# Splitting x's first block earlier, three values in an old constant tile, and weight decoding spread evenly after attention, in a fused attention and two-MLP kernel

## The chip, the cores and the metric

The kernel runs on one core of a Trainium2 chip. The metric is the device time of one execution in microseconds (us): the time before is the median of three runs, 884.39 us (883.90 to 886.73). About 0.3% is what a measurement of this kernel can tell from no change.

## The reference

Attention with a causal mask and a linear memory (4 batches, 8 heads, 576 tokens, 64 dimensions) makes a matrix x of 2304 tokens by 512. Two MLPs follow, everything in float32:

```python
x = attn_out.transpose(0, 2, 1, 3).reshape(B * S, H * D)   # 2304 x 512
h = x @ w_in                                               # 512 -> 2048
g = s * np.maximum(h, 0) ** 2 + b
y = g @ w_out                                              # 2048 -> 512
h = y @ w2_in                                              # 512 -> 1024
solu = h * softmax(h)
ln = (solu - mean) / sqrt(var + 1e-6) * g_ln
out = ln @ w2_out                                          # 1024 -> 512
```

## The kernel before, in words

**Products in three matmuls.** A float32 operand is split into a high part (fp32r, the faster matmul type) and a low rest. Each product is then three matmuls: high by high, low by high, high by low. In `hidden` (lines 420 to 438) the weights stand still in the array and x's parts `xh` and `xl` are streamed past them. In `ystep` (lines 602 to 610) weights stand still and `gh`, `gl` are streamed. In the second MLP it is `yh`/`yl` and `zh`/`zl` that stand still, and weights that are streamed (lines 665 to 667 and 728 to 730).

**Weights are decoded on the fly.** There are 48 weight tiles, numbered in the order of the list `order` (lines 114 to 118): w0 to w9 are the input and output weights of feature blocks f = 0 to 4, w10 to w31 are those of f = 5 to 15 in pairs (input of f, output of f), w32 to w39 belong to the second MLP's input, w40 to w47 to its output. `decode(n)` (lines 141 to 168) loads a tile, rebuilds its value in several integer steps (ACT line 152, DVE lines 153, 154, 156, 158, POOL line 159) and splits it (ACT line 163, DVE line 164). That is two ACT instructions, five on DVE, one on POOL and one load in SP's queue. `decode_to(n)` decodes up to tile n. Where the program calls it decides where in the order these instructions stand.

**Where tiles lie.** A pool is opened on the left side of the on-chip memory unless it says `side="right"`. Left, one behind the other: `const`, `wpA` (18 weight buffers), `dec`, the first part's pools, later `yT`, `yp` and the second MLP's pools. Right: attention's pools and, once attention is done, `wpB` (7 weight buffers), `xs2` (x, xh, xl of the second part) and `gs2` (r, gh, gl). `in_b` (line 135) says which weights go to `wpB`: w18 to w24 and w43 to w47. All others lie in `wpA`. In the built program every left tile behind `const` that a matmul reads begins at a multiple of 64 bytes, and every right one at 32 bytes past such a multiple.

**Stages.** Attention runs over 16 pairs of heads. Between its steps go pieces of the first part (`first_part`, f = 0 to 4 for each half batch of 288 tokens: five `h` tiles, then four `y` tiles, named h3_1_4 for batch 3, half 1, f = 4). What is left of it when attention ends, about 21 pieces, is emitted in the loop of lines 567 to 569, one decode behind each piece until tile 25. Then `second_part` runs f = 5 to 15 over five token blocks (four of 512 tokens, one of 256) in ten rounds: rounds 0 to 4 for f = 5 to 9, rounds 5 to 9 for f = 10 to 15. Each round loads its x (`load2`), splits it (`split_x`: four ACT and four DVE instructions), and alternates `hstep` and `ystep`. The decodes within rounds are spread by the lines 616 to 626. The second MLP ends the kernel.

**What sets the order.** The program is recorded in that order, and a scheduler (`schedule_with_timeline_sim=True`) then orders each engine's instructions by its own estimate of times. Each engine executes its list strictly in that order. `tc.issue_after(ins)` keeps an instruction from standing ahead of `ins` in that planning. Line 588 uses it: round 0's split may stand only behind the last ACT instruction of the first part (`lastact`, line 475). Line 630 allocates three tiles of one column for the first softmax of the second MLP in `const`.

Of the kernel before, what the change touches and what calls it, by code (L numbers as in the profile page):

```python
# [8 lines left out]
F32 = mybir.dt.float32  # L9
# [3 lines left out]
AF = mybir.ActivationFunctionType  # L13
# [4 lines left out]
P = 128  # L18
# [5 lines left out]
def attention_mlp_kernel(  # L24
# [9 lines left out]
    nc = tc.nc  # L34
# [65 lines left out]
    RA = 2 * FP1 + 8  # L100
    RB = 25 - RA
# [73 lines left out]
    def decode_to(n):  # L175
        while decoded[0] < min(n, NW):
            with tc.issue_after(mark[0]) if mark[0] else nullcontext():
                decode(decoded[0])
            decoded[0] += 1
# [235 lines left out]


    attended = [False]
    lastact = [None]

    def hidden(w, xh, xl, n, ps, r, gh, gl, square=False):  # L420

# [18 lines left out]
    def split_x(x, xh, xl):  # L440
        for c in range(NC):
            nc.scalar.activation(xh[:, c], x[:, c], AF.Copy)  # L442
            nc.vector.tensor_tensor(xl[:, c], x[:, c], xh[:, c].bitcast(F32), ALU.subtract)  # L443
# [3 lines left out]
    def first_part(b, pools):  # L447

        xs, gs, ys, _ = pools
        for sub in range(2):  # L450
            nm = f"{b}_{sub}"
            x = xbs[b][:, :, sub * N1:(sub + 1) * N1]
            xh = xs.tile([P, NC, N1], F32R, tag="xh", name=f"xh{nm}")
            xl = xs.tile([P, NC, N1], F32R, tag="xl", name=f"xl{nm}")
            split_x(x, xh, xl)
            gq = []
            for f in range(FP1):
                ps = pools[3][0].tile([P, 512], F32, tag="mh"[len(pools[3]) - 1], name=f"h{nm}_{f}")
                r = gs.tile([P, N1], F32, tag="r", name=f"r{nm}_{f}", bufs=2)
                g = gs.tile([P, 2, N1], F32R, tag="g", name=f"g{nm}_{f}")  # L460
                decode_to(f + 1)
                hidden(wtiles["in", f], xh, xl, N1, ps[:, 0:N1], r, g[:, 0], g[:, 1])
                gq.append(g)
                yield
            for c in range(NC):
                ps = pools[3][-1].tile([P, 512], F32, tag="m", name=f"y{nm}_{c}")
                o = ps[:, 0:N1]
                decode_to(2 * FP1)
                for f in range(FP1):
                    wc = [wtiles["out", f][:, t, c * P:(c + 1) * P] for t in range(2)]  # L470
                    nc.tensor.matmul(o, wc[0], gq[f][:, 0], start=(f == 0), stop=False)
                    nc.tensor.matmul(o, wc[1], gq[f][:, 0], start=False, stop=False)
                    nc.tensor.matmul(o, wc[0], gq[f][:, 1], start=False, stop=(f == FP1 - 1))
                y = ys.tile([P, N1], F32, tag="y", name=f"yo{nm}_{c}")
                lastact[0] = nc.scalar.activation(y, o, AF.Copy).ins
                t0 = b * S + sub * N1
                nc.sync.dma_start(yd[:, c, t0:t0 + N1], y)
                yield
# [19 lines left out]
    with ExitStack() as fctx:  # L498
        xp = fctx.enter_context(tc.tile_pool(name="xp", bufs=2))
        xs = fctx.enter_context(tc.tile_pool(name="xs", bufs=1))  # L500
        gs = fctx.enter_context(tc.tile_pool(name="gs", bufs=FP1 + 1))
        ys = fctx.enter_context(tc.tile_pool(name="ys", bufs=2))
        ps_m = fctx.enter_context(tc.tile_pool(name="ps_m", bufs=2, space=PSUM))
        fpools = [xs, gs, ys, [ps_m]]
        filler = []
        with ExitStack() as actx:
            at = Attention(actx, xp)
            NS = CF + 1
            G = NU * NS
            at.load(0, "kq")  # L510
            warm_up(16)
            load_gate()
            at.load(1, "kq")
            at.load(0, "q", "z", "v")
            at.phi(0)
            at.load(1, "q", "v")
            load_consts()
            LAG = 2
            FG = NPAIR * NS + LAG + 1
            debt = 0.0  # L520
            tiles_of = lambda i: (2 * i, 2 * i + 1) if i < CF else (2 * CF,)
            for g in range(G + LAG):
                u, i = divmod(g, NS)
                if g < G and i != 1:
                    at.scores(u, *((0, 1) if i == 0 else (i,)))
                if g < 4:
                    with tc.issue_after(at.last):
                        warm_up(6)
                if i == CF and u < NU:
                    at.load(u + 2, "kq")  # L530
                if i == 3 and u < NU:
                    at.load(u + 2, "q")
                    at.load(u + 1, "z")
                if i == 2 and 0 < u < NU:
                    at.phi(u)
                if i == 3 and u < NU:
                    at.gates(u)
                if i == CF and u < NU:
                    at.weigh(u)
                if 0 <= g - LAG:  # L540
                    lu, li = divmod(g - LAG, NS)
                    for t in tiles_of(li):
                        at.transposes(lu, t)
                    if li == CF - 1:
                        at.recip_t(lu)
                        at.phi_t(lu)
                    if li == CF:
                        at.values(lu)
                        at.load(lu + 2, "v")
                        if lu % NPAIR == NPAIR - 1:  # L550
                            filler.append(first_part(lu // NPAIR, fpools))
                decode_to(min(int(g / 3.4), RA))
                if filler and g >= FG:
                    debt += 0.93 * 6 * (FP1 + NC) / (G - FG)
                    while debt >= 1 and filler:
                        debt -= 1
                        if next(filler[0], 0) == 0:
                            filler.pop(0)
        wpools[1] = ctx.enter_context(tc.tile_pool(name="wpB", bufs=RB, side="right", reuse_waits="tile"))
        xs2 = pctx.enter_context(tc.tile_pool(name="xs2", bufs=1, side="right", reuse_waits="tile"))  # L560
        gs2 = pctx.enter_context(tc.tile_pool(name="gs2", bufs=2, side="right", reuse_waits="tile"))
        ps_y = pctx.enter_context(tc.tile_pool(name="ps_y", bufs=1, side="right", space=PSUM, reuse_waits="tile"))
        ps_h = pctx.enter_context(tc.tile_pool(name="ps_h", bufs=2, side="right", space=PSUM, reuse_waits="tile"))
        fpools[3] = [ps_h, ps_m]
        load2(0, False)
        attended[0] = True
        for it in filler:
            for _ in it:
                decode_to(min(decoded[0] + 1, RA + RB))

    def second_part():
        load2(0, True)
# [4 lines left out]
        for ri, (fs, bi) in enumerate(rounds):  # L577
# [7 lines left out]
            x = xq.pop(ri)  # L585
            xh = xs2.tile([P, NC, NB], F32R, tag="xh", name=f"xh2_{ri}")
            xl = xs2.tile([P, NC, NB], F32R, tag="xl", name=f"xl2_{ri}")
            with tc.issue_after(lastact[0]) if ri == 0 else nullcontext():
                split_x(x[:, :, 0:n], xh[:, :, 0:n], xl[:, :, 0:n])
            ys = [ps_y.tile([P, 512], F32, tag=f"y{c}", name=f"y2_{ri}_{c}") for c in range(NC)]  # L590
            gq = {}

# [19 lines left out]
            for i, f in enumerate(fs):  # L612
                hstep(f)
                if i >= 1:
                    ystep(fs[i - 1])
                step += 1
                if ri == 0:
                    decode_to(min(decoded[0] + 2, g2))
                elif ri < len(blocks):

                    decode_to(g2 + (late - g2) * step // steps)
                elif ri < last:

                    decode_to(late + (last2 - late) * step // steps)
                else:
                    decode_to(decoded[0] + 1)
                if ri == last and i == 2:

                    z = dec.tile([P, WN, 2], I32, tag="raw", name="z0").rearrange("p n t -> p (n t)").bitcast(F32)
                    first["z"] = weights_of(0, z, *(const.tile([P, 1], F32, name=f"t0_{k}") for k in range(3)))  # L630
            if ri == last:
                decode_to(NW)
                first[1] = products(1)
# [36 lines left out]
    def weights_of(t, z, mx, sm, mu):  # L670

        hh = products(t) if t not in first else first.pop(t)
        nc.vector.tensor_reduce(mx, hh, AX.X, ALU.max, negate=True)
        nc.scalar.activation(z, hh, AF.Exp, bias=mx, accum_out=sm)
        nc.vector.tensor_scalar(sm, sm, 1e-9, None, ALU.add)
        nc.vector.reciprocal(sm, sm)
        nc.vector.scalar_tensor_tensor(z, hh, sm, z, ALU.mult, ALU.mult, accum_out=mu)
        return z, mu
# [119 lines left out]
```

## Time and profile before

| | before |
|---|---|
| median of 3 runs | 884.39 us |
| the profiled execution | 885.48 us |
| its span, first to last instruction | 883.7 us |
| PE (matmul) busy | 850.8 us, 96% of the span |
| DVE busy | 539.9 us, 61% |
| ACT busy | 513.7 us, 58% |
| POOL busy | 182.8 us, 21% |
| mean granted TensorE clock | 0.997 |

The span is 1.8 us shorter than the execution's own time. "Busy" of PE is a modelled figure: matmuls overlap, and the last one's end is estimated. So the text counts from the start of one matmul to the start of the next. "Idle before" in a row names what released the engine.

### The profile page before, as it was taken

To read this page: it belongs to the slowest core of one execution; us is meant where nothing else is said; L and a number is where in the kernel's file an instruction comes from. 1 tells how busy PE (TensorE), PEld (TensorE's weight loads), DVE (VectorE), ACT (ScalarE), POOL (GpSimd) and SP (SyncE) were. 2 spreads that over 40 slices of the span, in tenths; PEclk is the share of its full clock that TensorE was granted. 3 is DMA by queue.
4 is the path that set the end of the run, shared out by engine and by line. 5 is a ranking of instruction groups with operands and counts; after the bars stand their busy time and mean duration, and the time that the engine had idled before them with its cause. 6 is when DMAs were issued, how large, how long until landed. Compare 5 with 4: busy or idle time off the path is not lost.

```text
span 883.7 us, 14245 instructions
## 1 busy us (share of the span) xinstructions
PE 850.8 (96%) x5344; PEld 699.0 (79%) x5344; DVE 539.9 (61%) x1236; ACT 513.7 (58%) x1094; POOL 182.8 (21%) x180
## 2 busy tenths in 40 slices
PE   7899889999999999899999999999999999999997
PEld 5677668888878878878888888888988888888885
DVE  3898986768778467922338864454775444454532
ACT  4776765666666665555558776556774333433332
POOL 4445351332333222200002311101120000000000
PEclk9999999999999999999999999999999999999999
DMA  7445242533343204472013422111200000000000
GB/s 228 133 148 184 79 155 59 155 97 119 115 149 118 69 1 156 147 263 95 3 45 114 144 100 96 48 48 55 89 24 1 25 25 23 13 24 24 25 25 36
DMA packets 41494, 76.44 MB, mean 86 GB/s; under 512 B 6352, under 2 KB 20176, under 8 KB 41424
## 3 DMA queue, kind: packets, MB, share of 16 engines
q1 hardware_dynamic: 41424, 75.52, 26.5%
q8 instruction: 42, 0.69, 0.3%
q14 instruction: 28, 0.23, 0.1%
HBM read 61.35 MB, written 14.16 MB: 85 GB/s over the span
## 4 chain that ended last, share of the span: by engine, by line
PE 78%; DVE 13%; ACT 3%; issue 2%; POOL 1%; DMA 1%; POOLq 0%; SPq 0%; ACTq 0%; DVEq 0%
PE h L424 7%; PE h L425 7%; PE h L426 7%; PE y L609 5%; PE y L608 5%; PE y L610 5%; PE h L665 4%; PE h L666 4%; PE h L667 4%; PE o L730 4%; PE o L729 4%; PE o L728 4%; PE pp L372 3%; PE s L315 3%; PE po L404 3%
## 5 line engine op out<-in xcount | busy, mean ns | idle before, releaser
L425 PE MATMUL h<-xl,w 128*128 128x512 f32 (+2 forms) x380 | 131.0, 345 | 2.1 <-DVE xl L443 2.1
L159 POOL TENSOR_TENSOR wa<-wa,raw 128x512 f32<-128x512 f32 x48 | 67.8, 1415 | 314.5 <-DVE raw L158 198.2
L424 PE MATMUL h<-xh,w 128*128 128x512 f32 (+2 forms) x380 | 130.0, 349 | 2.8 <-ACT xh L442 2.5
L426 PE MATMUL h<-xh,w 128*128 128x512 f32 (+2 forms) x380 | 129.2, 341 | 0.0
L427 ACT ACTIVATE r<-h 128x512 f32<-128x512 f32 (+2 forms) x95 | 45.6, 489 | 87.3 <-PE h L426 73.0
L298 ACT ACTIVATE pr<-pr,mx 128x128 f32<-128x128 f32 (+3 forms) x128 | 70.8, 555 | 37.5 <-DVE mx L331 37.5
L432 DVE TENSOR_TENSOR gl<-r,gh 128x512 fp32r<-128x512 f32 (+1 forms) x55 | 37.2, 685 | 88.1 <-ACT r L431 88.0
L424 PEld LDWEIGHTS h<-xh,w 128*128 128x128 f32 x380 | 70.9, 188 | 15.2 <-ACT xh L442 3.5
L425 PEld LDWEIGHTS h<-xl,w 128*128 128x128 f32 x380 | 71.5, 188 | 13.1 <-DVE xl L443 3.8
L608 PE MATMUL y<-gh,w 128*128 128x512 f32 (+1 forms) x220 | 80.8, 372 | 0.0
L609 PE MATMUL y<-gh,w 128*128 128x512 f32 (+1 forms) x220 | 80.8, 372 | 0.0
L426 PEld LDWEIGHTS h<-xh,w 128*128 128x128 f32 x380 | 71.5, 188 | 8.1 <-issue 0.4
L331 DVE CUSTOM_DVE_ANT_0 pr<-s,big 128x128 f32<-128x128 f32 (+3 forms) x128 | 56.2, 485 | 9.6 <-PE s L315 9.2
L375 ACT ACTIVATE pt<-pp 128x256 f32<-128x256 f32 (+2 forms) x96 | 47.2, 518 | 22.5 <-PE pp L372 22.0
L610 PE MATMUL y<-gl,w 128*128 128x512 f32 (+1 forms) x220 | 60.0, 372 | 0.0
L728 PE MATMUL o<-w,zh 128*128 128x512 f32 x144 | 56.8, 395 | 0.8 <-ACT zh L722 0.8
L730 PE MATMUL o<-w,zl 128*128 128x512 f32 x144 | 56.9, 395 | 0.6 <-DVE zl L723 0.6
L667 PE MATMUL h<-w,yl 128*128 128x512 f32 x144 | 56.6, 393 | 0.0
L729 PE MATMUL o<-w,zh 128*128 128x512 f32 x144 | 56.6, 393 | 0.0
L665 PE MATMUL h<-w,yh 128*128 128x512 f32 x144 | 56.6, 393 | 0.0
L666 PE MATMUL h<-w,yh 128*128 128x512 f32 x144 | 56.6, 393 | 0.0
L315 PEld LDWEIGHTS s<-kq 64*128 64x128 f32 x640 | 40.1, 187 | 19.3 <-issue 6.7
(142 smaller groups left out, 1959.1 us busy)
## 6 DMA issues: line engine op xcount, KB each, us to landing
raw<-in_moe_w_in_dram SPq DMA_DIRECT2D x24, 512.0 KB, 3.8
raw<-in_moe_w_out_dram SPq DMA_DIRECT2D x24, 512.0 KB, 3.5
kq<-in_kq_dram SPq DMA_DIRECT2D x16, 608.0 KB, 4.0
xr<-xd SPq DMA_DIRECT2D x8, 1024.0 KB, 5.9
q<-in_q_dram SPq DMA_DIRECT2D x16, 320.0 KB, 3.0
v<-in_v_dram SPq DMA_DIRECT2D x16, 320.0 KB, 3.1
xd<-xb SPq DMA_DIRECT2D x4, 1152.0 KB, 6.5
yd<-yo SPq DMA_DIRECT2D x32, 144.0 KB, 2.4
```

The lines of the kernel that those rows point to most:

```text
L424: nc.tensor.matmul(ps, wc[0], xh[:, c, 0:n], start=(c == 0), stop=False)
L425: nc.tensor.matmul(ps, wc[0], xl[:, c, 0:n], start=False, stop=False)
L426: nc.tensor.matmul(ps, wc[1], xh[:, c, 0:n], start=False, stop=(c == NC - 1))
L608: nc.tensor.matmul(o, wc[0], gh[:, 0:n], start=(f == fs[0]), stop=False)
L609: nc.tensor.matmul(o, wc[1], gh[:, 0:n], start=False, stop=False)
L610: nc.tensor.matmul(o, wc[0], gl[:, 0:n], start=False, stop=(f == fs[-1]))
L665: nc.tensor.matmul(o, yh[:, c], w[:, 0], start=(c == 0), stop=False)
L666: nc.tensor.matmul(o, yh[:, c], w[:, 1], start=False, stop=False)
L667: nc.tensor.matmul(o, yl[:, c], w[:, 0], start=False, stop=(c == NC - 1))
L728: nc.tensor.matmul(oo, zh, w[:, 0], start=(f == 0), stop=False)
L729: nc.tensor.matmul(oo, zh, w[:, 1], start=False, stop=False)
L730: nc.tensor.matmul(oo, zl, w[:, 0], start=False, stop=(f == NF2 - 1))
```

## The change

```diff
@@ -415,7 +415,6 @@
     attended = [False]
-    lastact = [None]
 
@@ -472,7 +471,7 @@ first_part
                 y = ys.tile([P, N1], F32, tag="y", name=f"yo{nm}_{c}")
-                lastact[0] = nc.scalar.activation(y, o, AF.Copy).ins
+                nc.scalar.activation(y, o, AF.Copy)
@@ -564,9 +563,11 @@
         attended[0] = True
+        turn = 0
         for it in filler:
             for _ in it:
-                decode_to(min(decoded[0] + 1, RA + RB))
+                turn += 1
+                decode_to(min(decoded[0] + (turn % 4 == 0), RA + RB))
@@ -585,8 +586,7 @@ second_part
-            with tc.issue_after(lastact[0]) if ri == 0 else nullcontext():
-                split_x(x[:, :, 0:n], xh[:, :, 0:n], xl[:, :, 0:n])
+            split_x(x[:, :, 0:n], xh[:, :, 0:n], xl[:, :, 0:n])
@@ -615,10 +615,11 @@
                 if ri == 0:
-                    decode_to(min(decoded[0] + 2, g2))
+                    decode_to(decoded[0] + step % 2)
+                    early = decoded[0]
                 elif ri < len(blocks):
-                    decode_to(g2 + (late - g2) * step // steps)
+                    decode_to(early + (late - early) * step // steps)
@@ -627,7 +628,7 @@
                     z = dec.tile([P, WN, 2], I32, tag="raw", name="z0").rearrange("p n t -> p (n t)").bitcast(F32)
-                    first["z"] = weights_of(0, z, *(const.tile([P, 1], F32, name=f"t0_{k}") for k in range(3)))
+                    first["z"] = weights_of(0, z, *(gate[:, k:k + 1] for k in range(3)))
```

Three things are done. Round 0's split loses its bond to the end of the first part. The decodes w18 to w34 are placed differently: one behind every fourth piece of the first part's rest instead of one behind every piece, three in round 0 instead of none, and w26 to w34 evenly over rounds 1 to 4 instead of w25 to w34 from the seventh of their twenty steps on. And the three one-column tiles of line 630 become columns of `gate`, which attention no longer needs. Such a tile takes 32 bytes of each partition in `const`, so every left tile behind it now begins 96 bytes earlier, at 32 past a multiple of 64. Right tiles stay where they were, so tiles of both sides now begin alike.

Up to the end of attention the order of all engines is as before. In the fences below, a line of the program before is one or two higher or lower than in the changed one (its line 441 is line 442 before).

ACT just behind attention, before (wa18 is tile 18's first decode step, r3_0_0 takes h3_0_0 out of its accumulator):

```order
L435 ACTIVATE g2_1_4_4336<-r2_1_4_4335,b_sb_80 128x288
L152 ACTIVATE wa18_4355<-raw18_4353 128x512
L152 ACTIVATE wa19_4386<-raw19_4384 128x512
L152 ACTIVATE wa20_4417<-raw20_4415 128x512
L427 ACTIVATE r3_0_0_4500<-h3_0_0_4499 128x288
L427 ACTIVATE r3_0_1_4531<-h3_0_1_4530 128x288
```

and now (xr0 is the x of round 0, loaded back from memory):

```order
L434 ACTIVATE g2_1_4_4336<-r2_1_4_4335,b_sb_80 128x288
L152 ACTIVATE wa18_4412<-raw18_4410 128x512
L441 ACTIVATE xh2_0_4870<-xr0_4332 128x512 x4
L426 ACTIVATE r3_0_0_4452<-h3_0_0_4451 128x288
L426 ACTIVATE r3_0_1_4471<-h3_0_1_4470 128x288
```

Round 0's four splits now stand ahead of r3_0_0, in the place of two decode steps; before, they stood behind the first part's last instruction.

DVE in the last half batch, between the low parts g3_1_0 and g3_1_2 that the last `y` tiles wait for, before:

```order
L438 SCALAR_TENSOR_TENSOR g3_1_0_4706<-r3_1_0_4705,b_sb_80,g3_1_0_4706 128x288
L158 SCALAR_TENSOR_TENSOR raw22_4477<-raw22_4477 128x512
L158 SCALAR_TENSOR_TENSOR raw23_4518<-raw23_4518 128x512
L153 TENSOR_SCALAR wa24_4551<-wa24_4551 128x512
L434 SCALAR_TENSOR_TENSOR r3_1_2_4743<-r3_1_2_4743,s_sb_79 128x288
L154 SCALAR_TENSOR_TENSOR wa24_4551<-raw24_4549,wa24_4551 128x512
L156 TENSOR_SCALAR raw24_4549<-wa24_4551 128x512
L164 TENSOR_TENSOR w22_4486<-wa22_4479,w22_4486 128x512
L158 SCALAR_TENSOR_TENSOR raw24_4549<-raw24_4549 128x512
L438 SCALAR_TENSOR_TENSOR g3_1_1_4725<-r3_1_1_4724,b_sb_80,g3_1_1_4725 128x288
L438 SCALAR_TENSOR_TENSOR g3_1_2_4744<-r3_1_2_4743,b_sb_80,g3_1_2_4744 128x288
```

and now:

```order
L437 SCALAR_TENSOR_TENSOR g3_1_0_4658<-r3_1_0_4657,b_sb_80,g3_1_0_4658 128x288
L164 TENSOR_TENSOR w20_4605<-wa20_4598,w20_4605 128x512
L433 SCALAR_TENSOR_TENSOR r3_1_2_4707<-r3_1_2_4707,s_sb_79 128x288
L437 SCALAR_TENSOR_TENSOR g3_1_1_4677<-r3_1_1_4676,b_sb_80,g3_1_1_4677 128x288
L153 TENSOR_SCALAR wa21_4696<-wa21_4696 128x512
L437 SCALAR_TENSOR_TENSOR g3_1_2_4708<-r3_1_2_4707,b_sb_80,g3_1_2_4708 128x288
```

Seven decode steps stood between them, now two do.

PE where the first part meets round 0. Before, h2_0_5 began behind all of y3_1_3; now it stands between the products of y3_1_0 and y3_1_1:

```order
L472 MATMUL y3_1_1_4794<-g3_1_2_4708,w7_1378 128x288
L423 MATMUL h2_0_5_4884<-xh2_0_4870,w10_1959 128x512
L424 MATMUL h2_0_5_4884<-xl2_0_4871,w10_1959 128x512
L425 MATMUL h2_0_5_4884<-xh2_0_4870,w10_1959 128x512
L423 MATMUL h2_0_5_4884<-xh2_0_4870,w10_1959 128x512
L424 MATMUL h2_0_5_4884<-xl2_0_4871,w10_1959 128x512
L425 MATMUL h2_0_5_4884<-xh2_0_4870,w10_1959 128x512
L470 MATMUL y3_1_0_4763<-g3_1_3_4727,w8_1442 128x288
L471 MATMUL y3_1_0_4763<-g3_1_3_4727,w8_1442 128x288
```

So matmuls that need nothing from the first part stand where the products of g3_1_3 and g3_1_4 waited. On SP, the load of xr1 and the stores of y move ahead of the loads of raw21 to raw27, and no DMA is added.

## Rows read from the trace of the kernel before

In a view of stretches a row is: from and to in us from the span's start, its length, then busy us and number of instructions of PE, PE's weight loads, DVE, ACT and POOL, the granted TensorE clock (1.00 is 2.4 GHz, 0.50 is 1.2 GHz), the DMA engines' busy share and GB/s. In a view in order of time it is: start, duration, engine, line, operation, out and in, shapes, count, and in brackets the idle time before and its releaser.

**Rows 1.** Stretches: rest of the first part, round 0, most of the rest.

```profile
337.17:383.69 46.52, 42.33 (x290) 39.87 (x289) 37.93 (x66) 23.77 (x55) 10.98 (x7) 0.96 0.52 163
383.69:411.00 27.31, 26.02 (x110) 20.28 (x109) 6.72 (x11) 15.76 (x27) 0.00 (x0) 1.00 0.61 217
...
484.00:680.00 196.00, 196.00 (x924) 162.32 (x923) 118.39 (x200) 126.00 (x210) 27.40 (x20) 1.00 0.21 71
```

**Rows 2.** PE in order of time, 362 to 365 us: start of h3_1_2 and of h3_1_3.

```profile
362.79 0.30 PE L424 MATMUL h<-xh,w 128*128 128x288 f32 x1
...
364.38 0.30 PE L424 MATMUL h<-xh,w 128*128 128x288 f32 x1
```

**Rows 3.** PE in order of time, 339 to 484 us: waits and their neighbours.

```profile
339.83 0.53 PE L424 MATMUL h<-xh,w 128*128 128x288 f32 x2 [0.83 <-ACT xh L442]
...
344.38 0.40 PE L424 MATMUL h<-xh,w 128*128 128x288 f32 x1
...
357.78 0.40 PE L425 MATMUL h<-xl,w 128*128 128x288 f32 x1 [1.40 <-DVE xl L443]
...
376.12 0.52 PE L471 MATMUL y<-g,w 128*128 128x288 f32 x1 [1.07 <-ACT g L435]
...
384.92 0.74 PE L424 MATMUL h<-xh,w 128*128 128x512 f32 x2 [1.07 <-ACT xh L442]
...
482.35 0.39 PE L424 MATMUL h<-xh,w 128*128 128x512 f32 x1
483.41 0.50 PE L425 MATMUL h<-xl,w 128*128 128x512 f32 x1 [0.67 <-DVE xl L443]
```

**Rows 4.** Stretches: the one at the lower clock.

```profile
376.25:379.66 3.41, 3.15 (x13) 2.80 (x13) 1.14 (x3) 0.81 (x3) 0.00 (x0) 0.50 0.23 91
```

**Rows 5.** Stretches: ten microseconds of the first part's rest.

```profile
365.00:375.00 10.00, 9.58 (x69) 8.94 (x67) 9.97 (x15) 4.66 (x11) 4.92 (x3) 1.00 0.53 163
```

**Rows 6.** DVE in order of time, one step of a decode.

```profile
356.25 0.68 DVE L154 SCALAR_TENSOR_TENSOR wa<-raw,wa 128x512 int32<-128x512 int32 x1
```

**Rows 7.** ACT in order of time, 343 to 387 us.

```profile
343.92 0.71 ACT L427 ACTIVATE r<-h 128x288 f32<-128x288 f32 x2 [1.02 <-PE h L426]
...
384.25 2.18 ACT L442 ACTIVATE xh<-xr 128x512 fp32r<-128x512 f32 x4
```

**Rows 8.** The view of tile xr, 330 to 345 us: its load's issue and landing.

```profile
L493 SPq DMA_DIRECT2D xr<-xd x1: 567/567/567, 337.5 to 337.5; - x1
...
DMA to landing us min/median/max: 6.9/6.9/6.9
```

**Rows 9.** PE, h2_6_12 (w24, right) from 551.41, h2_6_13 (w26, left) from 554.14.

```profile
551.41 0.40 PE L424 MATMUL h<-xh,w 128*128 128x512 f32 x1
...
554.14 0.39 PE L424 MATMUL h<-xh,w 128*128 128x512 f32 x1
...
556.01 0.40 PE L608 MATMUL y<-gh,w 128*128 128x512 f32 x1
```

**Rows 10.** PE, second MLP: w41 from 709.71, w43 from 711.07, last matmul of w47.

```profile
709.71 0.39 PE L728 MATMUL o<-w,zh 128*128 128x512 f32 x1
...
711.07 0.40 PE L728 MATMUL o<-w,zh 128*128 128x512 f32 x1
...
714.35 0.39 PE L730 MATMUL o<-w,zl 128*128 128x512 f32 x1
```

**Rows 11.** PE, 256-token block: w14 from 472.47, w16 from 473.88, w18 from 478.47.

```profile
472.47 0.28 PE L424 MATMUL h<-xh,w 128*128 128x256 f32 x1
...
473.88 0.28 PE L424 MATMUL h<-xh,w 128*128 128x256 f32 x1
...
478.47 0.28 PE L424 MATMUL h<-xh,w 128*128 128x256 f32 x1
...
479.42 0.28 PE L426 MATMUL h<-xh,w 128*128 128x256 f32 x1
```

## The prediction, made before the changed kernel was run

> **What bounds the kernel now.** I read the stretches first. From 484 to 680 us PE is busy in all of its 196.00 us [rows 1], so in the later rounds only matmuls that run faster could save time. Two earlier stretches differ. From 337.17 to 383.69 us (the rest of the first part, from h2_1_4 on) PE issues 288 matmuls of 288 columns: 12 of h2_1_4, 36 of y2_1, ten h tiles of 12, eight y tiles of 15. One takes 0.1325 us from start to start, as the 12 of h3_1_2 show (364.38 - 362.79 = 1.59) [rows 2]. That is 38.2 us of 46.5, so 8.3 us are lost. In round 0, from 383.69 to 411.00, stand 108 matmuls of 512 columns (five h tiles and four y steps of 12). At 0.2338 us each [rows 9] that is 25.2 of 27.3 us, so 2.1 are lost.
>
> The PE rows in order of time say to whom [rows 3]: a wait for xh at 339.83, for xl at 357.78, for g at 376.12, for round 0's xh at 384.92, and much later, for xl, at 483.41. Behind the wait at 376.12 the granted clock is 0.50 (1.2 GHz) for 3.41 us [rows 4].
>
> The reason stands in DVE's row: from 365 to 375 it is busy 9.97 of 10 us [rows 5]. It is not that first-part work is too much for DVE; seven weight decodes (w18 to w24) stand in its list among it, each with five instructions of up to 0.68 us [rows 6], up to 3.4 us per decode. xl and g, for which PE waits, queue behind them. After that DVE rests in round 0 with 6.72 us busy of 27.31 [rows 1].
>
> **The change, part by part.**
>
> *The decodes.* DVE's list up to g3_1_4 now holds w18 to w21, three decodes fewer, so 10 us less of DVE work at 3.4 each; xl2_0's four instructions add about as much as one decode. ACT loses two instructions per decode there, POOL one, and SP one load ahead of stores. These 7 us of slack are more than the waits at 357.78 and 376.12 were long. w22 to w25 go into round 0, where DVE has 20 us free. w26 to w34 go evenly over rounds 1 to 4, one behind about every second of 20 steps. The order that the rounds need stays met: round 0 needs w10 to w19, which are there. If that cover were gone, ystep in round 0 would wait for a decode of 3.4 us; nothing in the list suggests it.
>
> *The early split.* Where g3_1_3 and g3_1_4 were waited for, PE now has h2_0_5 to do, and the wait for round 0's xh at 384.92 goes. So does the dip of the clock at 376.
>
> *What goes in all.* Of 8.3 us, the wait at 339.83 stays, since the order up to there is the same: 0.83 idle [rows 3] and a slow restart, 1.3. So 7.0 go. The 2.1 of round 0 go. At 482.35 two starts are 1.06 apart instead of 0.23 [rows 3]; 0.8 may go. Together **9.9 us**.
>
> *What comes.* ACT's list now has the four splits of xr0 ahead of r3_0_0. xr0's load is issued at 337.5 and lands 6.9 us later [rows 8], so at 344.4, and nothing in the change moves it. The four splits take 2.1 us (2.18 to the end of the last) [rows 7], then r3_0_0 and r3_0_1 follow; one takes 0.4 (two end 0.71 after the first's start) [rows 7]. So r3_0_0 is done at 344.4 + 2.1 + 0.4 = 346.9 and not at 344.3. PE's h3_0_2 needs the accumulator that r3_0_0 empties, and begins at 344.38 now [rows 3]; it will begin at 347.0. **2.6 us** are added, as one stall, and r3_0_1, yo2_1_0, yo2_1_1 and g3_0_0 queue behind it on ACT.
>
> A stall of 2.6 us is longer than any single wait of [rows 3]. Behind 376.12, the waits were 1.07 and shorter ones, and the clock fell; behind 357.78, with one wait of 1.40, no such row follows. I take it that the clock falls once: 3.41 us at half speed cost **1.7** [rows 4]. Bounds: 0, and 3.4 if it happens twice.
>
> What is left over I cannot read from before. I take one wait as long as the longest here, **1.4** [rows 3]. Bounds: 0, and half of what went, 4.9. So the transition gains 9.9 - 2.6 - 1.7 - 1.4 = **4.2 us**, at best 7.3, at worst nothing.
>
> *The moved buffers.* This is the larger part. Two neighbouring h tiles of round 6 have the same shape, both at full clock, with the same moved operands xh and xl on the right side. h2_6_12, whose weights w24 lie on the right too, issues 12 matmuls in 554.14 - 551.41 = 2.73 us, 0.2275 each. h2_6_13, whose w26 lies on the left, issues 8 in 556.01 - 554.14 = 1.87 us, 0.2338 each [rows 9]. The second MLP shows it with roles exchanged. There zh stands still on the left. With streamed w41 and w42, on the left too, 6 matmuls take 711.07 - 709.71 = 1.36 us, 0.2267 each; with w43 to w47, on the right, 14 take 714.35 - 711.07 = 3.28 us, 0.2343 each [rows 10]. So it goes neither by the line nor by the side of one operand, but by whether both operands lie alike. Before, left tiles begin at a multiple of 64 bytes and right ones 32 bytes past one. Now all begin 32 past, as the right-with-right pair does, so I expect 0.2275 everywhere.
>
> Mixed pairs of 512 columns: in rounds 0 to 4 four of five f have left weights, in rounds 5 to 9 three of six for `in` and four of six for `out`; with 12 matmuls each in four wide blocks that is (4 + 3) x 48 = 336 and (4 + 4) x 48 = 384. In the second MLP five of eight weight tiles lie right: 5 x 3 x 18 token tiles = 270. Together 990, by 0.0063 us = 6.2. I take that difference for all, since right-with-right is what all become; 0.0076 [rows 10] would give 7.5, and 0 is the other end. In the 256-token block it goes the other way: 0.1175 with left weights (12 from 472.47 to 473.88) against 0.1188 with right ones (8 from 478.47 to 479.42) [rows 11], so 180 matmuls lose 0.2. **6.0 us** are left. PE has no idle time in these stages, so they count in full; ACT, next busiest with 126 of 196 us [rows 1], is no new bound.
>
> The Trainium skill, "TensorE: Matmul & The Clock Gate", section "Step-by-step: what each phase is for", speaks against this term: TensorE has two independent read ports, and loading the next tile's weights takes nothing from the running matmul. By that rule, where operands lie could not matter and the sum would be 4.2; rows 9 and 10 show two speeds in the same stretch.
>
> *The columns of gate.* Three small results are written into a tile that nothing reads any more. The instructions are the same, so I cost them at nothing.
>
> **Sum.** 4.2 + 6.0 = 10.2 us. The profiled execution took 885.48 us and would take 875.3. The median of the runs is 884.39, 1.1 lower; there it is **874.2 us**. Its own range, from 7.3 + 7.3 to 1.5 + 4.5 us gained, is 870 to 878.
>
> **Rivals.**
>
> *Placement counts by side, not by address.* Both operands lying in the same half of the memory would explain rows 9 and 10 as well, since before the two go together everywhere. Then 96 bytes change nothing, and neither do they if the ports are as independent as the page says and the two speeds have another cause. The time is 884.4 - 4.2 = 880.2. For it: no row has a left and a right tile alike. Against: narrow matmuls go the other way [rows 11], which looks like a matter of phase between two streams more than of distance. 0.20.
>
> *The transition gains nothing.* The stall at 344 keeps ACT and DVE late to the end of the first part, and what went comes back as new waits for r and g. Then only the buffers count: 884.4 - 6.0 = 878.4. For it: ACT's list is strict and everything behind the splits waits for a DMA. Against: DVE has less to do by 7 us. 0.08.
>
> *Slower: the clock falls at the stall and stays low.* Place: from 347 us, when h3_0_2 starts. Price: half of each microsecond at 1.2 GHz. It decides from where it eats the gain of 10.2, in which 3.41 us of low clock are included, and 2.7 more: (10.2 + 2.7) x 2 + 3.4 = 29 us. If it held to where round 0 took over, 35 us, 16 more would be lost, and the time would be 884.4 - 10.2 + 15.8 = 890.0. For it: the stall is the longest wait, and first-part work comes in pieces that wait for each other. Against: the one low stretch ended after 3.41 us though PE then waited again [rows 3, 4]. 0.04.
>
> **How the numbers follow.** My forecast, both gains, has 0.68; the rivals have 0.20, 0.08 and 0.04. The range 871 to 881 leaves out the forecast's best edge, the slower rival and the upper edge of the first one. A measurement can tell 0.3%, 2.65 us, from no change. All but the last rival, and the worst edges of the first two, lie lower than 881.7: faster 0.91, same 0.05, slower 0.04.
>
> **What would show it.** In the changed profile, one wait of some 2.6 us before h3_0_2, released by ACT r or xh, with a clock of 0.50 behind it; no wait for g before y3_1; h2_0_5 ahead of y3_1_2; DVE no longer full from 365 to 375. In round 6, h2_6_13 should take 0.2275 per matmul like h2_6_12, and in the second MLP w43 like w41; the time from one token tile to the next shrinks by 0.1 us. If h2_6_13 still takes 0.234, the first rival holds. If the time from h3_0_0 to h2_1_5 (339.83 to 411.00 before, 71.2) is not some 4 us shorter, the second does.

## The result, and the profile after

| | before | after |
|---|---|---|
| median of 4 runs each, one chip | 884.89 us | 874.86 us (871.32 to 875.52) |
| ratio, with its 95% interval | 1 | 0.9876 [0.9845, 0.9908] |
| the profiled execution | 885.48 us | 874.54 us |
| its span | 883.7 us | 872.8 us |
| mean granted TensorE clock | 0.997 | 0.994 |

The changed kernel is faster by 1.2%, or 10.0 us. The forecast was 874.2 us, 871 to 881.

Stretches of the changed kernel, in the columns of [rows 1]: what is left of the first part up to round 0's first matmul, from there to round 1's first h tile, ten microseconds of the first part's rest, the two stretches at the lower clock, and most of the rest:

```profile
337.17:375.05 37.88, 34.30 (x241) 33.40 (x240) 27.94 (x52) 20.28 (x48) 5.62 (x4) 0.95 0.49 160
375.32:405.50 30.18, 30.18 (x153) 25.82 (x151) 14.98 (x25) 19.36 (x33) 4.05 (x4) 1.00 0.71 245
365.00:375.00 10.00, 10.00 (x77) 10.00 (x77) 7.42 (x13) 4.84 (x11) 1.94 (x2) 1.00 0.35 113
347.35:350.76 3.41, 3.41 (x16) 3.41 (x15) 2.87 (x7) 0.94 (x2) 1.23 (x1) 0.50 0.58 150
480.00:676.00 196.00, 196.00 (x941) 165.23 (x940) 112.52 (x194) 126.69 (x211) 24.35 (x19) 1.00 0.19 62
855.93:859.35 3.42, 3.42 (x10) 2.64 (x9) 0.14 (x1) 0.00 (x0) 0.00 (x0) 0.50 0.00 0
```

From 365 to 375 DVE has 7.42 us of work where it had 9.97 [rows 5], and PE has no idle time. In 196 us of the later rounds PE issues 941 matmuls where it issued 924 [rows 1], and has no idle time in either: they run faster. The clock falls at 347.35, and once more near the end; early in attention, at 16.26, it had also been at 0.50 for 3.41 us.

PE in order of time, the columns as in [rows 3]; the rows answer to those at 339.83, 344.38, 362.79, 384.92, 482.35 and 483.41 there, and the one at 405.50 is the h2_1_5 that began at 411.00:

```profile
339.10 0.40 PE L423 MATMUL h<-xh,w 128*128 128x288 f32 x1 [0.83 <-ACT xh L441]
...
346.37 0.40 PE L423 MATMUL h<-xh,w 128*128 128x288 f32 x1 [2.68 <-ACT r L426]
...
364.05 0.40 PE L423 MATMUL h<-xh,w 128*128 128x288 f32 x1
...
375.32 0.40 PE L423 MATMUL h<-xh,w 128*128 128x512 f32 x1
...
405.50 0.39 PE L423 MATMUL h<-xh,w 128*128 128x512 f32 x1
...
475.59 0.39 PE L423 MATMUL h<-xh,w 128*128 128x512 f32 x1
476.26 0.50 PE L424 MATMUL h<-xl,w 128*128 128x512 f32 x1 [0.28 <-DVE xl L442]
```

The waits for xl at 357.78, for g at 376.12 and for round 0's xh at 384.92 [rows 3] are gone. One new wait stands there, 2.68 us before h3_0_2. ACT's rows say why, in the columns of [rows 7]:

```profile
343.84 0.63 ACT L441 ACTIVATE xh<-xr 128x512 fp32r<-128x512 f32 x1 [2.79 <-DMA xr<-xd]
...
345.93 0.39 ACT L426 ACTIVATE r<-h 128x288 f32<-128x288 f32 x1
```

ACT waits for the load of xr0, splits it in 2.09 us, and only then empties the accumulator that h3_0_2 needs. From h3_0_0 to h2_1_5 it is 405.50 - 339.10 = 66.40 us where it was 71.17.

PE in round 6, as in [rows 9]: h2_6_12 from 542.94, h2_6_13 from 545.66 to 547.47:

```profile
542.94 0.39 PE L423 MATMUL h<-xh,w 128*128 128x512 f32 x1
...
545.66 0.39 PE L423 MATMUL h<-xh,w 128*128 128x512 f32 x1
...
547.47 0.39 PE L608 MATMUL y<-gh,w 128*128 128x512 f32 x1
```

h2_6_12 takes 2.72 / 12 = 0.2267 us per matmul, h2_6_13 1.81 / 8 = 0.2263, and the latter was the slow one of [rows 9] with 0.2338. The second MLP shows the same, as in [rows 10]: w41 from 698.93, w43 from 700.29, last matmul of w47.

```profile
698.93 0.39 PE L729 MATMUL o<-w,zh 128*128 128x512 f32 x1
...
700.29 0.39 PE L729 MATMUL o<-w,zh 128*128 128x512 f32 x1
...
703.46 0.39 PE L731 MATMUL o<-w,zl 128*128 128x512 f32 x1
```

With w43 to w47 one takes 3.17 / 14 = 0.2264 where it took 0.2343.

### The profile page after: what moved, and what is told of

Its sections match the earlier page's. It is cut to its first block, busy times and chain, and to the rows that moved or that the text cites. A ratio compares the mean times of both kernels' runs of the same rounds, so it can differ in the third digit from the quotient of the medians.

```text
span 872.8 us, 14240 instructions
## 1 busy us (share of the span) xinstructions
PE 845.0 (97%) x5344; PEld 702.5 (80%) x5344; DVE 535.4 (61%) x1236; ACT 513.7 (59%) x1094; POOL 180.0 (21%) x180
## 4 chain that ended last, share of the span: by engine, by line
PE 84%; DVE 7%; ACT 4%; DMA 2%; issue 2%; POOL 1%; POOLq 0%; SPq 0%; ACTq 0%
PE h L423 7%; PE h L424 7%; PE h L425 7%; PE y L609 5%; PE y L608 5%; PE y L610 5%; PE h L668 4%; PE h L666 4%; PE h L667 4%; PE o L731 4%; PE o L730 4%; PE o L729 4%; PE po L404 4%; PE pp L372 4%; PE s L315 3%; PE y L470 2%
## 5 line engine op out<-in xcount | busy, mean ns | idle before, releaser
L159 POOL TENSOR_TENSOR wa<-wa,raw 128x512 f32<-128x512 f32 x48 | 65.1, 1356 | 309.4 <-DVE raw L158 244.4
```

## The experiments: the moved buffers

Ratios are to the kernel before, run on the same chip, with 95% intervals. "Mixed" matmuls are those of 512 columns with one operand from the left side and one from the right. Their mean is taken from start to start over the whole trace, without those above 0.26 us (waits and low clock); in each kernel over 980 of the 990 are left.

**e1: the kernel before, with the columns of `gate` alone.** It separates the moved buffers from everything in the transition.

```diff
-                    first["z"] = weights_of(0, z, *(const.tile([P, 1], F32, name=f"t0_{k}") for k in range(3)))
+                    first["z"] = weights_of(0, z, *(gate[:, k:k + 1] for k in range(3)))
```

> The kernel before with the last edit alone: the three values of the second MLP's first softmax kept in columns of gate. The order of every engine stays as before; only the left tiles begin 96 bytes earlier. Address theory (left and right tiles now begin alike, so 990 matmuls of 512 columns fall from 0.234 to 0.227 us each): 6 us below the kernel before, ratio 0.993, and h2_6_13 as fast as h2_6_12. Side theory (left with right is slow wherever they begin): no change, ratio 1.000, h2_6_13 still at 0.234.

Measured: 878.16 us, 0.9928 [0.9913, 0.9943]. PE of this kernel in round 6, then in the transition:

```profile
545.93 0.39 PE L424 MATMUL h<-xh,w 128*128 128x512 f32 x1
...
548.65 0.39 PE L424 MATMUL h<-xh,w 128*128 128x512 f32 x1
...
550.47 0.39 PE L608 MATMUL y<-gh,w 128*128 128x512 f32 x1
```

```profile
337.75 0.40 PE L424 MATMUL h<-xh,w 128*128 128x288 f32 x1 [0.83 <-ACT xh L442]
...
355.69 0.40 PE L425 MATMUL h<-xl,w 128*128 128x288 f32 x1 [1.40 <-DVE xl L443]
...
374.00 0.61 PE L471 MATMUL y<-g,w 128*128 128x288 f32 x1 [1.07 <-ACT g L435]
...
382.85 0.50 PE L424 MATMUL h<-xh,w 128*128 128x512 f32 x1 [1.07 <-ACT xh L442]
...
408.26 0.39 PE L424 MATMUL h<-xh,w 128*128 128x512 f32 x1
```

h2_6_13 is at 1.82 / 8 = 0.2275 and the four waits that [rows 3] has in the transition are all there. So 96 bytes of address, with no instruction more or less, are worth 5.8 us by the medians. The rival that only the side counts falls.

**e2, e3, e4: the changed kernel with three, two, one unused tiles of one column.** They move the left buffers forward again by 96, 64 and 32 bytes, and nothing else. This is e3's edit; e2 has `range(3)`, e4 `range(1)`.

```diff
     warm = const.tile([P, 256], mybir.dt.bfloat16, name="warm")
+    for k in range(2):
+        const.tile([P, 1], F32, name=f"pad{k}")
```

> The changed kernel with three unused one-column tiles put back into const, so that left tiles begin where they began before; the new order of the work stays. Address theory: 6 us above the changed kernel, about 4.5 below the kernel before, ratio 0.995; mixed pairs at 0.234 again. Side theory: as the changed kernel, ratio 0.988.

> The changed kernel with two unused one-column tiles in const: left tiles move 64 bytes on and still begin 32 bytes past a multiple of 64, as the right ones do. If the place within 64 bytes counts, nothing changes: as the changed kernel, ratio 0.988, all pairs at 0.227. If the distance that the buffers were moved counts, or a larger unit than 64 bytes, some of the 6 us come back.

> The changed kernel with one unused one-column tile in const: left tiles move 32 bytes on and begin at a multiple of 64 again. If the place within 64 bytes counts: as with three tiles, 6 us above the changed kernel, ratio 0.995, mixed pairs at 0.234. If the distance moved counts: a third of the way, ratio about 0.990.

Measured: e2 879.11 us, 0.9938 [0.9920, 0.9956]; e3 878.68, 0.9934 [0.9918, 0.9950]; e4 879.39, 0.9947 [0.9932, 0.9962]. e2 and e4 came out as expected. **e3 did not:** its left and right buffers begin alike modulo 64 bytes, and it is as slow as the other two. PE of e3 in round 6:

```profile
545.75 0.39 PE L425 MATMUL h<-xh,w 128*128 128x512 f32 x1
...
548.50 0.40 PE L425 MATMUL h<-xh,w 128*128 128x512 f32 x1
...
550.36 0.39 PE L610 MATMUL y<-gh,w 128*128 128x512 f32 x1
```

h2_6_13 takes 1.86 / 8 = 0.2325. The reading of the prediction, 32 bytes past a multiple of 64, was therefore not the rule. In the compiled program the right buffers begin 224 bytes past a multiple of 256; the left ones 64 past before, 224 after, and 32 past in e3. Alikeness modulo 128 or more was still possible.

**e9, e10: one unused tile of 128 bytes, of 256 bytes** (e10 has `[P, 64]`).

```diff
+    const.tile([P, 32], F32, name="pad0")
```

> One unused constant of 128 bytes behind warm: left buffers begin 96 bytes past a multiple of 512, right ones 480 past one, alike modulo 128 and not modulo 256. In the run with two more tiles (alike modulo 64, not modulo 128) the mixed wide matmuls took 0.2334 us against 0.2271 of the changed kernel. Theory A, operands must begin alike modulo 128: 0.227, ratio .988, as the changed kernel. Theory B, modulo 256 or more: 0.233, ratio .993 to .995. Rival, the 96 bytes of gate did it in another way than by likeness: also 0.233.

> The same with 256 bytes: left 224 past a multiple of 512, right 480, alike modulo 256 and not modulo 512. Modulo 128 or modulo 256: mixed wide matmuls take 0.227 us, ratio .988. Modulo 512, or not by likeness: 0.233, ratio .993 to .995. A unit above 512 is excluded by the changed kernel itself, whose slices of weights begin 512 bytes from each other and all take 0.227.

Measured: e9 877.58 us, 0.9932 [0.9916, 0.9947]; e10 873.36 us, 0.9876 [0.9860, 0.9893]. PE in round 6, e9 and then e10:

```profile
543.75 0.40 PE L424 MATMUL h<-xh,w 128*128 128x512 f32 x1
...
546.51 0.40 PE L424 MATMUL h<-xh,w 128*128 128x512 f32 x1
...
548.37 0.39 PE L609 MATMUL y<-gh,w 128*128 128x512 f32 x1
```

```profile
543.18 0.39 PE L424 MATMUL h<-xh,w 128*128 128x512 f32 x1
...
545.90 0.39 PE L424 MATMUL h<-xh,w 128*128 128x512 f32 x1
...
547.71 0.39 PE L609 MATMUL y<-gh,w 128*128 128x512 f32 x1
```

All in one table; the offset is that of the left buffers, the right ones stay at 224:

| kernel | left offset modulo 256 | mixed matmul, mean |
|---|---|---|
| before | 64 | 0.2339 us |
| e4 | 0 | 0.2332 us |
| e3 | 32 | 0.2334 us |
| e2 | 64 | 0.2339 us |
| e9 | 96 | 0.2326 us |
| after | 224 | 0.2271 us |
| e10 | 224 | 0.2271 us |

Only where both operands begin alike modulo 256 is the mixed matmul fast; e1, with left buffers at 224 too, has 0.2270. It is not that 224 is a good place by itself: matmuls with both operands on the left take 0.2270 to 0.2277 us in every one of these kernels, wherever the left buffers begin. 64 and 128 bytes are excluded by e3 and e9. e10 excludes 512: its left buffers lie 256 bytes from where they are alike modulo 512, and it is as fast. What in the hardware works in steps of 256 bytes was not tried.

## The experiments: the transition

The four combinations of early or late split with spread or old decodes, all with the moved buffers, and two places between. The measure beside the ratio is the time from h3_0_0 to h2_1_5, which holds the whole transition.

**e5: the changed kernel with the split bound to the first part's end again.**

```diff
-                nc.scalar.activation(y, o, AF.Copy)
+                lastact[0] = nc.scalar.activation(y, o, AF.Copy).ins
...
-            split_x(x[:, :, 0:n], xh[:, :, 0:n], xl[:, :, 0:n])
+            with tc.issue_after(lastact[0]) if ri == 0 else nullcontext():
+                split_x(x[:, :, 0:n], xh[:, :, 0:n], xl[:, :, 0:n])
```

> The changed kernel with round 0's split bound to the first part's last ACT instruction again; decodes and addresses as in the changed kernel. My theory: the stall of 2.7 us before h3_0_2 and the low clock behind it (1.6 us) go, the waits for round 0's xh of about 1.1 and the one before y3_1_2 come back, 2 us together with their restarts and no decode on DVE to lengthen them; so about 2 us below the changed kernel, ratio 0.986. Rival, that the early split itself brings the transition's gain: 2 to 4 us above the changed kernel, ratio 0.991.

**e6: the changed kernel with the decodes where they were.**

```diff
-                decode_to(min(decoded[0] + (turn % 4 == 0), RA + RB))
+                decode_to(min(decoded[0] + 1, RA + RB))
...
-                    decode_to(decoded[0] + step % 2)
-                    early = decoded[0]
+                    decode_to(min(decoded[0] + 2, g2))
...
-                    decode_to(early + (late - early) * step // steps)
+                    decode_to(g2 + (late - g2) * step // steps)
```

> The changed kernel with the decodes placed as before: one behind each piece of the first part's rest, none in round 0. Early split and addresses as in the changed kernel. My theory: DVE is full again from 347 to 377 us, and waits for xl and g come back behind the stall, 2 to 5 us; ratio 0.991 to 0.994. Rival, that the decodes' place does not matter once round 0's work fills the gaps: as the changed kernel, ratio 0.988.

Measured: e5 871.45 us, 0.9854 [0.9836, 0.9871], as expected; e6 875.03 us, 0.9892 [0.9876, 0.9907], which is the value expected by the rival, that the decodes' place does not matter, and not mine. PE of e5, then of e6:

```profile
338.77 0.40 PE L424 MATMUL h<-xh,w 128*128 128x288 f32 x1 [0.83 <-ACT xh L442]
...
378.27 0.50 PE L424 MATMUL h<-xh,w 128*128 128x512 f32 x1 [1.07 <-ACT xh L442]
...
403.70 0.39 PE L424 MATMUL h<-xh,w 128*128 128x512 f32 x1
```

```profile
339.64 0.40 PE L423 MATMUL h<-xh,w 128*128 128x288 f32 x1 [0.83 <-ACT xh L441]
...
346.92 0.41 PE L423 MATMUL h<-xh,w 128*128 128x288 f32 x1 [2.71 <-ACT r L426]
...
376.50 0.40 PE L423 MATMUL h<-xh,w 128*128 128x512 f32 x1
...
406.90 0.39 PE L423 MATMUL h<-xh,w 128*128 128x512 f32 x1
```

From h3_0_0 to h2_1_5, with e1 as the fourth:

| | old decodes | spread decodes |
|---|---|---|
| late split | 70.51 us (e1) | 64.93 us (e5) |
| early split | 67.26 us (e6) | 66.40 us (after) |

The two halves of the change do not add. Spreading the decodes is worth 5.6 us with the late split and 0.9 with the early one. The early split is worth 3.3 us with the old decodes, and costs 1.5 once they are spread. With the early split PE has round 0's matmuls to issue where it would wait for DVE, so a crowded DVE costs little; with DVE free most of those waits are gone anyway (e5 keeps the 1.07 us before round 0), and what is left of the early split is its price.

That price is the clock more than the stall before h3_0_2. In e1, e6 and the changed kernel the granted clock fell to 0.50 for 3.41 us within the stretch, in e5 it did not. e9 (below) has the changed kernel's order and its stall, but kept the full clock: there the stretch takes 403.95 - 338.57 = 65.38 us, with mixed matmuls that are still slow (0.66 us here, by e1 against before). So the stall alone costs about what e5's remaining waits cost, and the 1.5 us are those of the low clock; they are also part of the 5.6 us between e1 and e5. By their medians the changed kernel and e5 can't be told apart, since the intervals overlap.

**e7, e8: the split bound to a place between.** e7 binds it to the last output copy recorded by turn 13 of the first part's rest, e8 to that by turn 5; otherwise the edit is e5's, with `midact` in place of `lastact[0]`.

```diff
                 turn += 1
+                if turn == 13:
+                    midact = lastact[0]
```

> The changed kernel with round 0's split bound to the ACT instruction that ends y3_0_2, in the middle of the last half batch: behind the landing of its load, ahead of the end of the first part. My theory: the stall before h3_0_2 (2.7 us) and its low clock (1.6 us) go and nothing comes in their place: 4 us below the changed kernel, ratio 0.983. Rival, that the time lost there was slack of DVE's list anyway: as the changed kernel, ratio 0.988.

> The changed kernel with round 0's split bound to the ACT instruction that ends y2_1_3: 8 us later than in the changed kernel, behind the landing of its load, but still ahead of r3_0_3 and r3_0_4. My theory: the stall before h3_0_2 goes, but the four splits, 2.1 us, stand ahead of the two r that h3_1 and y3_0 wait for, so a wait of up to 2 us comes before y3_0_0, without a low clock; 1 to 3 us below the changed kernel, ratio 0.985 to 0.987. If the landing alone was the matter: as with the split in the middle of the last half batch, 0.983.

Measured: e7 869.51 us, 0.9829 [0.9811, 0.9847], as expected; e8 871.38 us, 0.9849 [0.9827, 0.9871], with the expected wait but also with a low clock, which was not expected. PE of e7, then of e8:

```profile
338.88 0.40 PE L424 MATMUL h<-xh,w 128*128 128x288 f32 x1 [0.83 <-ACT xh L442]
...
343.44 0.41 PE L424 MATMUL h<-xh,w 128*128 128x288 f32 x1
...
370.68 0.40 PE L424 MATMUL h<-xh,w 128*128 128x512 f32 x1
...
401.06 0.39 PE L424 MATMUL h<-xh,w 128*128 128x512 f32 x1
```

```profile
339.12 0.40 PE L424 MATMUL h<-xh,w 128*128 128x288 f32 x1 [0.83 <-ACT xh L442]
...
357.47 0.40 PE L471 MATMUL y<-g,w 128*128 128x288 f32 x1 [2.06 <-ACT g L435]
...
404.96 0.39 PE L424 MATMUL h<-xh,w 128*128 128x512 f32 x1
```

In e7 the splits start at 363.9, the stall is gone, h2_0_5 still comes early, and the stretch takes 62.18 us: 4.2 less than after, which has both the stall and the low clock. e7's interval lies below that of e10, which has the changed kernel's order, so it beats both kernels. In e8 the splits start at 351.2, and the wait has moved to y3_0_0, for g, with the clock at 0.50 from 358.40; 65.84 us. The early split's price is thus a matter of what stands behind it on ACT.

## Why the prediction was right, point by point

- **What goes.** Counted as start to start above the back-to-back pitch (0.133 us with 288 columns), the stretch from 337 us to h2_1_5 had 10.27 us too much before. 1.42 of them, around h3_0_0, stayed, so 8.85 went; the wait at 482 shrank by 0.4. Together 9.3 against 9.9.
- **The stall.** Forecast 2.6, from the load's landing and four splits. It is 2.68 of idle time, and 2.95 with the slow restart. The mechanism, and the row that releases it, are as the prediction said.
- **The low clock.** Forecast 1.7. It fell at 347.35 for 3.41 us. What that costs can be read from e9, whose stall is as long and whose clock stayed. Its rows are h3_0_0, the first matmul behind the stall (h3_0_2), h3_1_2 and h2_1_5:

```profile
338.57 0.40 PE L424 MATMUL h<-xh,w 128*128 128x288 f32 x1 [0.83 <-ACT xh L442]
...
345.83 0.40 PE L424 MATMUL h<-xh,w 128*128 128x288 f32 x1 [2.66 <-ACT r L427]
...
362.03 0.40 PE L424 MATMUL h<-xh,w 128*128 128x288 f32 x1
...
403.95 0.40 PE L424 MATMUL h<-xh,w 128*128 128x512 f32 x1
```

```profile
345.83:362.03 16.20, 16.20 (x120) 15.99 (x121) 14.94 (x29) 9.13 (x23) 3.03 (x2) 1.00 0.50 167
```

The same 120 matmuls take 16.20 us there and 364.05 - 346.37 = 17.68 after: 1.5 for the low clock. The rival in which it stays low is refuted: in every kernel here in which it fell in the transition, it was back after 3.41 us.
- **What is left over.** Forecast 1.4, taken from the longest wait since no row told; 0.2 was left. This was the worst-sized term of the sum. The transition gained 9.3 - 2.95 - 1.5 - 0.2 = 4.6 us; the forecast was 4.2. The lower edge under the prediction's sum, 1.5 + 4.5 us gained, does not follow from the terms: at their bounds the transition would lose 1.0 (9.9 - 2.6 - 3.4 - 4.9), and the buffers would bring nothing.
- **The moved buffers.** Forecast 6.0. e1 measured 5.8 us by medians, and its interval is 5.0 to 7.7 us. By the pitches it is a little more: 990 x (0.2339 - 0.2271) = 6.7 for the mixed ones. Of the others of 512 columns, 336 with both operands on the right gained 0.0012 each (0.2283 to 0.2271) and 594 with both on the left 0.0003 (0.2273 to 0.2270): 0.6 that the prediction did not have. The both-right pairs did not move against each other, so the likeness of a pair alone does not explain their gain; its cause stays open. The 256-token block lost 180 x 0.0020 = 0.4 (means of 0.1177 and 0.1197): the sign of [rows 11], and twice the 0.2 forecast. Together that is 6.9, within e1's interval.
- **The step that failed** was one of reasoning, not of the sum: that it is enough to begin 32 bytes past a multiple of 64. Left and right also became alike modulo 256 with the same edit, and the trace of before could not tell the two. e3 did. That the time came out right is luck in this point: both readings say 0.227 for this change.
- **Not forecast:** the low clock from 855.93 to 859.35, behind the last waits, where before it stayed up until 881. At half speed 3.41 us cost this execution at most 1.7. e10 has it too; e5 and e7 do not while PE still works. The spread from 871.32 to 875.52 us goes with the clock: three executions have a mean granted clock of 0.994, the one of 871.32 us has 1.000. So there the clock did not fall behind the stall, and the forecast's 1.7 us is a price that not every execution pays.

The Trainium skill, "TensorE: Matmul & The Clock Gate", section "Step-by-step: what each phase is for", says that the streamed operand and the weight load have independent read ports, so that loading weights takes nothing from the running matmul. By that alone the mixed matmuls would have one speed wherever their operands lie; e1 against before shows two: the same instructions at other addresses go from a mean of 0.2339 us to one of 0.2270. Whether it is the weight load that takes something there, no run shows.

The prediction put one gain to split and decodes together. The table of four shows that the two do not add: once the decodes are spread, the early split gains nothing, costs the low clock's 1.5 us where the clock falls, and 4.2 us against e7's place for it.

## What to carry to other kernels

Where two shapes that should run alike differ by a few per cent, compare the addresses of both operands before looking for a wait: here unused bytes decide 0.6% of the kernel. That is shown for matmuls of 512 columns alone. Two cures of one stall must be tried apart, since each may take the other's gain and leave its own price. Work that waits for a load goes on an in-order engine's list behind what others wait for, and not ahead of it, but early enough to be ready when its reader is.

## What the runs showed that I had not expected

- **Likeness modulo 256 bytes.** Mixed wide matmuls take 0.227 us when both operands begin alike modulo 256, and 0.2326 to 0.2339 when they don't. Mixed matmuls of 256 columns go the other way: 0.1197 when alike, and 0.1176 (e3) to 0.1192 (e9) when they aren't.
- **The clock is not told by the length of the wait.** Seven kernels here have the early split's stall. After idle times of 2.64 (e3), 2.65 (e10), 2.68 (after), 2.71 (e6) and 2.83 us (e4) the clock fell to 0.50; after 2.48 (e2) and 2.66 us (e9) it did not. In the kernel before it fell behind a wait of 1.07 us [rows 3, 4], and in e5, with the same 1.07 us before round 0, it did not. One kernel differs from execution to execution as well: two of e8's have a mean granted clock of 1.000 and take 869.63 and 870.33 us, two have 0.998 and take 872.43 and 873.05.
- **A full engine need not cost anything.** In e7 DVE is busy 9.93 of the 10 us from 365 to 375, as it was before [rows 5], and PE has no idle time there:

```profile
365.00:375.00 10.00, 10.00 (x66) 9.38 (x66) 9.93 (x19) 6.76 (x15) 1.79 (x1) 1.00 0.52 147
```
